# Where tasks stand in a hand-written order: weight fetches, word sums and splits between three fused stages

## The chip, the cores and the metric

One Trainium2 chip, one of its cores. The metric is the device time of one execution in microseconds (us); the kernel before was run three times, and its median is what the changed kernel is compared with.

## The reference, cut to what matters

Decayed linear attention over 12 blocks (written as chunks of 128 tokens in the kernel), then two MLPs on its 1536 x 512 output:

```
x   = attention(q, k, v, lam)                    # 2 batches x 768 tokens, 8 heads of 64
h   = x @ w_in                                    # 512 -> 2048
x   = (s * relu(h)**2 + b) @ w_out                # 2048 -> 512           (MLP1)
xn  = x / sqrt(mean(x*x) + 1e-6) * rms_g
x   = (silu(xn @ w_gate) * (xn @ w_val)) @ w_out  # 512 -> 1536 -> 512    (MLP2)
```

The weights come as 64-bit numbers.

## The kernel before, in words

**Words.** A weight piece is fetched as raw 64-bit words into one of two rooms (`stage[0]`, `stage[1]`, by SP's queue, line 116). ScalarE makes a float from the upper word (`scale_word`, L123) and reads the low word (`low_word`, L129); VectorE shifts (L135) and adds the two (`sum_words`, L140). Then a matrix is split into a high part (`split_hi`, ScalarE, L143) and a low part (`split_lo`, VectorE, L146), and each product is three matmul passes (`PASSES`), hi x hi, hi x lo, lo x hi.

**Seven products.** The first matmul of each MLP is done in quads: a weight pair `j` and a half of the tokens (batch) `s`, as Strassen-Winograd 2 x 2 blocks with seven products instead of eight. Sums of weight blocks (S1 to S4) are made on GpSimd (L218 to L221), sums of x blocks (T1 to T4) on VectorE (L267); all are split. A quad is five parts with a `yield` after each; the additions between products are VectorE's (L306, `add`). A product that goes on top of a bank can start only after the addition that reads the bank. The weights 0 and 1 of MLP1 use eight plain products (`hplain`).

**Tasks.** `w_tasks(j, after)` gives the tasks of one weight pair in order: `first` (scale and low word of the first half, then `after(0)`, which issues the fetch of the next pair's first half), `second`, `third` (then `after(1)`), `sums_hi` (GpSimd's four sums, then the split of blocks that need no sum), `first_lo` (their low part, then ScalarE's split of S1 to S4) and `second_lo` (two low parts). Weights 0 and 1 of MLP1 have five tasks (`plain_hi`, `plain_lo` at the end); weights 2 to 7 seven (`fourth` and `first_hi` apart). `x_tasks` gives t1 to t4 and the high and low part of each x block (hB11, lB11, ...).

All engines work through their instructions in the order in which the program issues them; that order is written by hand. Three mechanisms set it:

- In the attention, `plan[g]` says which tasks are issued after chunk `g`'s outputs, then `load_chunk(g + 4)` issues that chunk's q, k, v. All loads and fetches are issued on SP's queue, in this order; a fetch waits there until its room has been read.
- In MLP1's first matmul, `plan[(i, part)]` says which tasks follow part `part` of quad `i`; MLP2's first matmul has another such plan.
- Between them, MLP1's second matmul runs over 16 f tiles for each of two token halves (`blk`): step `it` makes the `y_product` and `z_product` of f tile m for four columns d. The operand of tile m is split three steps ahead (`r_hi(m + 3)`, `r_lo(m + 3)`) into one of four rooms. In the second half, the list `todo` holds the tasks for MLP2: weights 8 and 9, 18 x tasks, weights 10 and 11; `work(n)` issues the next n of them. Only the first 12 f tiles run in this loop; the last four run column by column (`for d in range(NK)`), so that each column's `square` (ScalarE) and `take1` (VectorE) follow while the next column is computed.

In MLP2's loop over quads, `work()` is called after the parts 1, 3 and 4 and issues one task of `todo` each.

Of the kernel before, what the change touches and what calls it, by code (L numbers as in the profile page):

```python
# [22 lines left out]
def attention_moe_moe2_kernel(  # L23
# [83 lines left out]
    def work(n=1):  # L107
        for _ in range(min(n, len(todo))):
            todo.pop(0)()
# [327 lines left out]
    with tc.tile_pool(name="att", bufs=1) as att:  # L437
# [20 lines left out]
        NPRE = 4  # L458
        nc.vector.memset(ones, 1.0)
        row = att.tile([1, H + 2], F32, name="row")  # L460
        nc.scalar.dma_start(row[:, 0:H], lam.rearrange("(o h) -> o h", o=1))
        load_qk(0)
        load_qk(1)
        load_v(0)
# [137 lines left out]
        prepare(0)  # L602
        def after_w(j):
            def load(part):
                if j + 1 < 2:
                    load_w(j + 1, part)

            return load

# [3 lines left out]
        def spread_s():  # L613
# [3 lines left out]
            nc.vector.tensor_copy(params[:, H : H + 2], pps[:, 0:2])  # L617

        plan = {
            3: w0[0:1], 4: w0[1:2], 5: w0[2:4] + [xt["hB11"]],  # L620
            6: [xt["lB11"]], 7: [xt["hB21"]] + w0[4:5], 8: [xt["lB21"], xt["hB12"]],
            9: [xt["lB12"], xt["hB22"]], 10: [xt["lB22"]] + w1[0:1], 11: w1[1:2] + [spread_s],
        }
        for g in range(NG):
            if (g + 1) % NCH == 0 and g + 1 < NG:
                prepare_state(g + 1)
            if g + 1 < NG:
                prepare(g + 1)
            if g % NCH:
                prepare_state(g)  # L630
            if g == NG - 1:

                quad0 = hquad(0)
                next(quad0)
                next(quad0)
            st = outputs(g)
            add_state(g, st)
            scores(g + 2)
            for t in plan.get(g, ()):
                t()  # L640
            load_chunk(g + NPRE)
            if g == 1:
                load_w(0, 0)
                load_w(0, 1)
            if g == 8:
                nc.sync.dma_start(g_col, rms_g.rearrange("(k p) -> p k", p=P))
                nc.sync.dma_start(row[:, H : H + 1], s.rearrange("(o h) -> o h", o=1))
                nc.sync.dma_start(row[:, H + 1 : H + 2], b.rearrange("(o h) -> o h", o=1))
# [19 lines left out]

        return load

    load_w(2, 0)
    load_w(2, 1)
    wt = {j: w_tasks(j, next_w(j)) for j in range(2, NPR)}
    wo = {f: out1_tasks(f) for f in range(NF1)}

# [10 lines left out]
    def r_lo(m):  # L686
# [14 lines left out]
        (3, 0): [ut["lT3"], wt[2][4]],  # L701
        (3, 1): [wt[2][5]],
        (3, 2): [wt[2][6]],
        (3, 3): [wt[3][0]],
        (4, 0): [ut["hT4"]],
        (4, 1): [ut["lT4"]],
    }
    for ts, slots in (
        (wt[3][1:], ((4, 1), (4, 2), (4, 3), (5, 1), (5, 2), (5, 3))),
        (wt[4], ((5, 4), (6, 1), (6, 2), (6, 3), (7, 1), (7, 2), (7, 3))),  # L710
        (wt[5], ((7, 4), (8, 1), (8, 2), (8, 3), (9, 1), (9, 2), (9, 3))),
        (wt[6], ((9, 4), (10, 1), (10, 1), (10, 2), (10, 3), (10, 4), (11, 1))),
# [75 lines left out]
    for blk in range(B):  # L788
# [42 lines left out]
            take(d, xq[blk][:, d, BT:BW], acc2[d // 2][:, d % 2 * BX : (d % 2 + 1) * BX])  # L831


        by_f = NF1 if blk == 0 else NF1 - 4
        for it in range(by_f):
            m = NF1 * blk + it
            if m == 0:
# [24 lines left out]
            if it == 0:  # L862
                norm_total(0)
                m_u0[0] = piece(early, "u0a", 12)
                ops2.append([x_place(m_u0[1], i) for i in range(5)] + [x_place(m_u0[0], i) for i in range(2)])

                def next_w2(j):
                    def load(part):
                        if j + 1 < NPR + NF2:
                            load_w(j + 1, part)  # L870

                    return load

                w2 = [w_tasks(NPR + f, next_w2(NPR + f)) for f in range(NF2)]
                xt = x_tasks(xq[0], ops2[0], xq[1])
                todo += w2[0] + w2[1] + [xt[k] for k in X_ORDER] + w2[2] + w2[3]
            if it == 1:
                norm_rstd(0, bank(0, "nps0"))
            if it in (3, 4):
# [1 line left out]
                norm_apply(0, slice(h * HB, (h + 1) * HB), bank(1 - h, f"rb0_{h}")[:, 0:HB])()  # L881
            work(1)
            r_lo(m + 3)
            work((0, 0, 1, 1, 2, 2, 4, 4, 4, 4, 3, 1)[it])
        if blk == 0:
            for d in (0, 2):
                take1(d)
# [4 lines left out]
                square(NK + d)  # L892
            for d in range(NK):
                take2(d)
    r_hi(2 * NF1 - 1)
    r_lo(2 * NF1 - 1)
    for d in range(NK):
        for m in range(2 * NF1 - 4, 2 * NF1):
            y_product(m, d)
        for m in range(2 * NF1 - 4, 2 * NF1):  # L900
            z_product(m, d)
        square(d)
        if d == 0:
            work(2)
        take1(d)
        if d == 1:
            square(NK)
            square(NK + 1)
            take2(0)
            take2(1)  # L910
            work(1)
        if d == 2:
            work(len(todo))
            norm_pair(1, 0)


# [116 lines left out]
    def spread():  # L1033
# [5 lines left out]
        (0, 0): [lambda: square(NK + 2), lambda: square(NK + 3), lambda: take2(2), lambda: take2(3)],  # L1039
        (0, 1): [lambda: norm_pair(1, 2)],  # L1040
        (0, 2): [lambda: norm_pairs(1)],
        (0, 4): [lambda: norm_rstd(1, bank(1, "nps1"))],
        (1, 3): [spread],
        (1, 4): [lambda: scale[1]()],
        (2, 0): [xt["t1"], xt["hB11"]],
        (2, 1): [xt["t2"], xt["lB11"]],
        (2, 2): [xt["hT2"], xt["t3"]],
        (2, 3): [xt["lT2"], xt["hT3"]],
        (2, 4): [xt["hT1"]],
        (3, 0): [xt["lT3"]],  # L1050
        (3, 1): [xt["lT1"], xt["hB21"]],
        (3, 2): [xt["t4"]],
        (3, 3): [xt["hT4"], xt["lB21"]],
        (3, 4): [xt["hB22"]],
        (4, 0): [xt["lT4"]],
        (4, 1): [xt["lB22"]],
        (23, 1): [lambda: split_first(0)],
    }
    work(len(todo))
    for i in range(len(order)):  # L1060
        for part, _ in enumerate(quad(i)):
            for t in plan.get((i, part), ()):
# [123 lines left out]
```

## Time and profile before

| | |
|---|---|
| median of 3 runs | 614.34 us (614.27 to 614.41) |
| the profiled execution | 614.62 us; its span, first to last instruction, 612.7 us |
| TensorE busy | 592.5 us, 97% of the span |
| VectorE, ScalarE, GpSimd busy | 67%, 53%, 18% |
| mean granted clock of TensorE | 0.988 |

Times in the rows below are microseconds from the span's start. A row of the timeline can hold several like instructions (xN); in brackets stands how long the engine was idle before it and who ended that. PE is TensorE, DVE VectorE, ACT ScalarE, POOL GpSimd, SPq SP's queue. PEclk is the granted clock of TensorE, 1.00 for 2.4 GHz and 0.50 for 1.2 GHz. Durations on PE overlap their neighbours; the distance of two starts is the time that the work takes.

### The profile page before, as it was taken

Reading aid. Unit: us, or ns where it says so; the run is one execution under the profiler, and the core shown is the slowest. Engines: PE = TensorE matmul, PEld = TensorE weight load, DVE = VectorE, ACT = ScalarE, POOL = GpSimd, SP = SyncE. Lnnn points to the kernel's source line nnn. Section 1 sums busy time; section 2 is a strip of 40 time slices with the busy share of each in tenths; the row PEclk is TensorE's granted clock in tenths of the full one; section 3 lists DMA queues with packets and bytes.
Section 4 is the critical chain, followed back from the end, with each engine's and each line's share of the span. In section 5 each row is a group of like instructions: output and inputs, shape, how many; then the busy total and the mean of one; then the engine's idle time right before and its main releaser. Section 6 shows DMA issues by size and latency. Waiting matters only on the chain.

```text
span 612.7 us, 9214 instructions
## 1 busy us (share of the span) xinstructions
PE 592.5 (97%) x3590; PEld 546.0 (89%) x3590; DVE 408.9 (67%) x654; ACT 322.7 (53%) x572; POOL 111.8 (18%) x118
## 2 busy tenths in 40 slices
PE   8999799999999999999979989999999999999997
PEld 7888699999998888888858989999999998888886
DVE  5684785777777776668856696777777777875200
ACT  5674686678776664534643243444444445764200
POOL 3551021121122332032130100222222200000000
PEclk9999799999999999999979999999999999999999
DMA  8982102222232332112220001222222221330300
GB/s 324 339 301 70 35 34 70 70 70 74 92 110 74 135 138 68 35 35 68 69 69 1 2 1 35 76 80 85 70 68 70 70 68 58 115 103 1 137 35 35
DMA packets 17282, 51.98 MB, mean 85 GB/s; under 512 B 2390, under 2 KB 2390, under 8 KB 17238
## 3 DMA queue, kind: packets, MB, share of 16 engines
q1 hardware_dynamic: 17236, 51.39, 24.5%
q8 instruction: 28, 0.46, 0.3%
q14 instruction: 16, 0.13, 0.1%
q10 hardware_dynamic: 2, 0.00, 0.0%
HBM read 48.24 MB, written 3.15 MB: 84 GB/s over the span
## 4 chain that ended last, share of the span: by engine, by line
PE 81%; DVE 8%; ACT 4%; issue 2%; DMA 2%; POOL 1%; SPq 0%; DVEq 0%; ACTq 0%; POOLq 0%
PE q L295 26%; PE out L1078 16%; PE h L295 15%; PE y L794 11%; PE z L806 6%; PE o L557 1%; PE sc L515 1%; PE o L566 1%; DVE u_None L140 1%; DMA st_None<-in_w_dram 1%; ACT u_None L143 1%; DMA k<-in_kT_dram 1%; PE st L583 1%; DVE u_None L146 1%; DVE st_None L146 1%
## 5 line engine op out<-in xcount | busy, mean ns | idle before, releaser
L143 ACT ACTIVATE u_None<-u_None 128x768 fp32r<-128x768 f32 (+2 forms) x50 | 43.1, 870 | 52.8 <-DVE u_None L140 44.3
L295 PE MATMUL q<-u0b_None,u_None 128*128 128x384 f32 x360 | 68.6, 336 | 0.0
L295 PEld LDWEIGHTS q<-u0b_None,u_None 128*128 128x128 f32 x360 | 62.7, 188 | 0.9 <-DVE st_None L306 0.7
L146 DVE TENSOR_TENSOR u_None<-u_None,u_None 128x512 fp32r<-128x512 f32 (+1 forms) x66 | 53.7, 837 | 11.4 <-ACT u_None L143 11.4
L218 POOL TENSOR_TENSOR u_None<-u_None 128x256 f32<-128x256 f32 x18 | 19.7, 1094 | 208.8 <-DVE u_None L140 184.0
L123 ACT ACTIVATE u_None<-st_None 128x512 f32<-128x512 f32 x68 | 45.2, 665 | 19.7 <-issue 12.9
L295 PE MATMUL q<-xs_None,u_None 128*128 128x384 f32 x288 | 55.2, 334 | 0.0
L140 DVE CUSTOM_DVE_ANT_0 u_None<-u_None 128x1024 uint16<-128x1024 uint16 x68 | 47.3, 696 | 10.3 <-ACT u_None L129 5.3
L295 PEld LDWEIGHTS q<-xs_None,u_None 128*128 128x128 f32 x288 | 50.4, 188 | 0.0
L129 ACT ACTIVATE u_None<-st_None 128x512 uint32<-128x512 uint16 x68 | 45.2, 665 | 6.9 <-DVE u_None L146 5.9
L306 DVE TENSOR_TENSOR st_None<-q,r_None 128x384 f32<-128x384 f32 x48 | 26.6, 554 | 20.8 <-PE q L295 20.7
L972 ACT ACTIVATE st_None<-r_None 128x384 f32<-128x384 f32 x24 | 12.6, 526 | 45.8 <-DVE r_None L306 45.8
L135 DVE TENSOR_SCALAR u_None<-u_None 128x512 uint32<-128x512 uint32 x68 | 32.9, 484 | 1.1 <-ACT u_None L123 0.7
L1078 PE MATMUL out<-u_None,xs_None 128*128 128x512 f32 x144 | 32.8, 389 | 0.0
L1078 PEld LDWEIGHTS out<-u_None,xs_None 128*128 128x128 f32 x144 | 27.0, 188 | 5.6
L295 PE MATMUL q<-u0a_None,u_None 128*128 128x384 f32 x144 | 29.0, 336 | 1.7 <-DVE st_None L306 1.7
L295 PE MATMUL h<-u0b_None,st_None 128*128 128x384 f32 x126 | 26.2, 355 | 4.2 <-DVE st_None L146 2.3
L1085 DVE COPY st_None<-out 128x512 f32<-128x512 f32 x4 | 2.8, 692 | 40.9 <-PE out L1078 40.9
L424 POOL TENSOR_TENSOR wsum_None<-wsum_None,u_None 128x512 f32<-128x512 f32 x15 | 20.6, 1372 | 49.1 <-DVE u_None L140 49.1
L295 PEld LDWEIGHTS h<-u0b_None,st_None 128*128 128x128 f32 x126 | 23.5, 202 | 5.2 <-DVE st_None L146 2.6
L295 PEld LDWEIGHTS q<-u0a_None,u_None 128*128 128x128 f32 x144 | 25.2, 188 | 2.4 <-DVE st_None L306 2.4
L295 PE MATMUL q<-g_None,u_None 128*128 128x384 f32 x144 | 26.9, 334 | 0.0
(202 smaller groups left out, 1317.3 us busy)
## 6 DMA issues: line engine op xcount, KB each, us to landing
st_None<-in_w_dram SPq DMA_DIRECT2D x68, 512.0 KB, 3.3
kv<-in_kv_dram SPq DMA_DIRECT2D x12, 512.0 KB, 7.4
q<-in_qT_dram SPq DMA_DIRECT2D x12, 256.0 KB, 6.5
k<-in_kT_dram SPq DMA_DIRECT2D x12, 256.0 KB, 7.0
out_dram<-st_None SPq DMA_DIRECT2D x8, 256.0 KB, 2.2
out_dram<-u_None SPq DMA_DIRECT2D x4, 256.0 KB, 2.6
row<-in_lam_dram ACTq DMA_DIRECT2D x1, 0.0 KB
g_col<-in_rms_g_dram SPq DMA_DIRECT2D x1, 2.0 KB, 6.5
```

Source lines behind the costliest of these rows:

```text
L123: nc.scalar.activation(m, t[:, :, 1].bitcast(F32), AF.Prelu, scale=2.0**-112, alpha=-(2.0**32))
L129: nc.scalar.activation(to.bitcast(U32), low, AF.Copy, scale=2.0**-13)
L135: nc.vector.tensor_scalar(m, m, 3, None, op0=ALU.logical_shift_left)
L140: nc.vector.tensor_tensor(m, m, t.bitcast(U32), op=ALU.add)
L143: nc.scalar.activation(to, src, AF.Copy)
L146: nc.vector.tensor_tensor(to, src, hi.bitcast(F32), op=ALU.subtract)
L295: nc.tensor.matmul(ps, ws[:, wi, wop * KC + kt * P : wop * KC + (kt + 1) * P], xs[xop][:, xi, kt, :], start=n == 0 and not more, stop=n == ...
L306: nc.vector.tensor_tensor(to, ps, more, op=ALU.add)
L424: nc.gpsimd.tensor_tensor(wsum, wsum, m, op=ALU.add)
L794: nc.tensor.matmul(acc[d], wt[:, wi, d * P : (d + 1) * P], gt[:, gi, 0:BT], start=it == 0 and pi == 0, stop=it == NF1 - 1 and pi == 2,)
L806: nc.tensor.matmul(acc2[d // 2][:, d % 2 * BX : (d % 2 + 1) * BX], wt[:, wi, d * P : (d + 1) * P], gt[:, gi, BT:BW], start=it == 0 and pi ...
L1078: nc.tensor.matmul(ps, rows_[:, ai], w_out[f][:, wi, :], start=first and pi == 0, stop=last and pi == 2)
```

## The change

- lam is loaded on SP's queue instead of ScalarE's, ahead of all other loads.
- In the attention, the fetch of weight 0 moves from after chunk 1 to after chunk 4, and its tasks to chunks 6 to 9; the splits of x blocks move to chunks 4 to 10.
- The fetch of weight 2 was issued behind the attention, ahead of the third task of weight 1 (`w1[2]`) which reads the same room; now the tasks of weight 1 issue it themselves, each half after its room has been read.
- In MLP1's first matmul, T4's split and the tasks of weight 3 move one or more parts later.
- In MLP1's second matmul, the loop takes 13 f tiles and the rows by column three. The x tasks alternate with the tasks of weight 10, three x tasks and one weight task at a time; the number of tasks for each step becomes 2 (steps 0 to 5 and 12) or 4 (steps 6 to 11), one for each of the columns 0, 1 and 2, and one task of 42 is left for MLP2's loop.
- In MLP2's first matmul, the x tasks of the second token half move one part later each.

```diff
-        nc.scalar.dma_start(row[:, 0:H], lam.rearrange("(o h) -> o h", o=1))
+        nc.sync.dma_start(row[:, 0:H], lam.rearrange("(o h) -> o h", o=1))
...
-                if j + 1 < 2:
-                    load_w(j + 1, part)
+                load_w(j + 1, part)
...
         plan = {
-            3: w0[0:1], 4: w0[1:2], 5: w0[2:4] + [xt["hB11"]],
-            6: [xt["lB11"]], 7: [xt["hB21"]] + w0[4:5], 8: [xt["lB21"], xt["hB12"]],
-            9: [xt["lB12"], xt["hB22"]], 10: [xt["lB22"]] + w1[0:1], 11: w1[1:2] + [spread_s],
+            4: [xt["hB11"]], 5: [xt["lB11"], xt["hB21"]], 6: [xt["lB21"]] + w0[0:1], 7: [xt["hB12"]] + w0[1:2],
+            8: [xt["lB12"]] + w0[2:4], 9: [xt["hB22"]] + w0[4:5], 10: [xt["lB22"]] + w1[0:1], 11: w1[1:2] + [spread_s],
         }
...
-            if g == 1:
+            if g == 4:
                 load_w(0, 0)
                 load_w(0, 1)
...
-    load_w(2, 0)
-    load_w(2, 1)
...
-        (3, 3): [wt[3][0]],
-        (4, 0): [ut["hT4"]],
-        (4, 1): [ut["lT4"]],
+        (4, 1): [ut["hT4"]],
+        (4, 2): [ut["lT4"]],
     }
     for ts, slots in (
-        (wt[3][1:], ((4, 1), (4, 2), (4, 3), (5, 1), (5, 2), (5, 3))),
+        (wt[3], ((4, 2), (4, 3), (4, 3), (4, 4), (5, 1), (5, 2), (5, 3))),
...
-        by_f = NF1 if blk == 0 else NF1 - 4
+        by_f = NF1 if blk == 0 else NF1 - 3
...
-                todo += w2[0] + w2[1] + [xt[k] for k in X_ORDER] + w2[2] + w2[3]
+                todo += w2[0] + w2[1]
+                for i, t in enumerate(w2[2]):
+                    todo += [xt[k] for k in X_ORDER[3 * i : 3 * i + 3]] + [t]
+                todo += w2[3]
...
             work(1)
             r_lo(m + 3)
-            work((0, 0, 1, 1, 2, 2, 4, 4, 4, 4, 3, 1)[it])
+            work(1 if it < 6 or it > 11 else 3)
...
-    r_hi(2 * NF1 - 1)
-    r_lo(2 * NF1 - 1)
     for d in range(NK):
-        for m in range(2 * NF1 - 4, 2 * NF1):
+        for m in range(2 * NF1 - 3, 2 * NF1):
             y_product(m, d)
-        for m in range(2 * NF1 - 4, 2 * NF1):
+        for m in range(2 * NF1 - 3, 2 * NF1):
             z_product(m, d)
         square(d)
-        if d == 0:
-            work(2)
         take1(d)
+        if d < 3:
+            work()
         if d == 1:
             square(NK)
             square(NK + 1)
             take2(0)
             take2(1)
-            work(1)
         if d == 2:
-            work(len(todo))
             norm_pair(1, 0)
...
         (0, 2): [lambda: norm_pairs(1)],
+        (0, 3): [work],
...
-        (2, 0): [xt["t1"], xt["hB11"]],
-        (2, 1): [xt["t2"], xt["lB11"]],
-        (2, 2): [xt["hT2"], xt["t3"]],
-        (2, 3): [xt["lT2"], xt["hT3"]],
-        (2, 4): [xt["hT1"]],
-        (3, 0): [xt["lT3"]],
-        (3, 1): [xt["lT1"], xt["hB21"]],
...
+        (2, 0): [xt["hB11"]],
+        (2, 1): [xt["t1"]],
+        (2, 2): [xt["lB11"], xt["t2"]],
+        (2, 3): [xt["hT2"], xt["t3"]],
+        (2, 4): [xt["lT2"], xt["hT3"]],
+        (3, 0): [xt["hT1"]],
+        (3, 1): [xt["lT3"]],
+        (3, 2): [xt["lT1"], xt["hB21"]],
...
-    work(len(todo))
     for i in range(len(order)):
```

## Rows read from the trace of the kernel before

**Rows 1.** The page: busy time, share and instructions of each engine.
```profile
PE 592.5 (97%) x3590; PEld 546.0 (89%) x3590; DVE 408.9 (67%) x654; ACT 322.7 (53%) x572; POOL 111.8 (18%) x118
```

**Rows 2.** Stretches: length, busy us (x instructions) per engine, PEclk, DMA share, GB/s.
```profile
57.50:75.46 17.96, 13.72 (x60) 13.08 (x61) 11.26 (x15) 12.32 (x20) 0.74 (x1) 0.81 0.19 59
...
305.41:330.23 24.82, 20.54 (x99) 16.77 (x98) 13.80 (x19) 11.30 (x16) 6.20 (x7) 0.86 0.14 44
```

**Rows 3.** Timeline, MLP1's last f tiles: start, length, engine, line, operation [idle before].
```profile
301.23 2.91 PE L794 MATMUL y<-st_None,xs_None 128*128 128x512 f32 x12
...
308.14 1.06 ACT L143 ACTIVATE u_None<-u_None 128x1024 fp32r<-128x1024 f32 x1 [2.13 <-POOL u_None L221]
309.11 0.83 ACT L143 ACTIVATE st_None<-u_None 128x768 fp32r<-128x768 f32 x1
...
309.98 0.51 PE L794 MATMUL y<-st_None,g_None 128*128 128x512 f32 x1 [3.03 <-ACT st_None L143]
...
330.23 2.25 PE L295 MATMUL q<-u0b_None,u_None 128*128 128x384 f32 x12
```

**Rows 4.** Timeline, VectorE and TensorE before and in MLP2's first quads.
```profile
326.36 1.28 DVE L146 TENSOR_TENSOR u_None<-u_None,u_None 128x512 fp32r<-128x512 f32 x2
...
335.15 0.55 DVE L306 TENSOR_TENSOR st_None<-q,r_None 128x384 f32<-128x384 f32 x1
...
338.24 1.39 PE L757 MATMUL nps<-ones,xq_None 128*128 128x1 f32 x12
...
355.10 1.32 PE L295 MATMUL q<-u0a_None,u_None 128*128 128x384 f32 x6 [1.58 <-DVE st_None L306]
```

**Rows 5.** Timeline, MLP1's first quad of seven products and its next.
```profile
100.53 1.32 PE L295 MATMUL h<-u0a_None,u_None 128*128 128x384 f32 x6 [0.99 <-DVE u_None L306]
...
102.83 1.20 PE L295 MATMUL h<-xs_None,u_None 128*128 128x384 f32 x6
...
103.87 2.24 PE L295 MATMUL h<-g_None,u_None 128*128 128x384 f32 x12
```

**Rows 6.** Timeline, MLP1's first quads: the last pieces of weight 1.
```profile
61.35 0.66 ACT L129 ACTIVATE u_None<-st_None 128x512 uint32<-128x512 uint16 x1 [0.95 <-DMA st_None<-in_w_dram]
...
63.88 0.61 PE L295 MATMUL h<-u0b_None,st_None 128*128 128x384 f32 x2 [1.92 <-ACT st_None L143]
...
66.81 3.57 PE L295 MATMUL h<-u0b_None,st_None 128*128 128x384 f32 x10 [2.32 <-DVE st_None L146]
```

**Rows 7.** Timeline, attention.
```profile
19.98 1.09 PE L557 MATMUL o<-prob,kv 128*64 128x128 f32 x16
...
23.80 1.09 PE L557 MATMUL o<-prob,kv 128*64 128x128 f32 x16
...
24.82 0.42 SPq L445 DMA_DIRECT2D k<-in_kT_dram  x1
...
30.38 1.16 PE L515 MATMUL sc<-q,k 64*128 64x128 f32 x16 [0.58 <-DMA k<-in_kT_dram]
...
34.78 1.06 ACT L143 ACTIVATE u_None<-u_None 128x1024 fp32r<-128x1024 f32 x1 [3.76 <-DVE u_None L140]
...
50.39 2.35 PE L295 MATMUL h<-u0b_None,u_None 128*128 128x384 f32 x12
```

**Rows 8.** Groups by line, 8 to 50.4 us: xcount | busy us, mean ns | idle.
```profile
L534 ACT ACTIVATE kdec<-kv,dec 128x64 f32<-128x64 f32 x80 | 20.0, 336 | 5.5 <-DVE dec L487 5.4
L517 DVE TENSOR_TENSOR prob<-sc,dec 128x512 f32<-128x512 f32 x24 | 15.5, 686 | 1.5 <-PE sc L515 0.7
...
L577 ACT ACTIVATE xq_None<-o 128x512 f32<-128x512 f32 x11 | 6.5, 589 | 6.5 <-PE o L566 6.5
...
L140 DVE CUSTOM_DVE_ANT_0 u_None<-u_None 128x1024 uint16<-128x1024 uint16 x2 | 1.4, 692 | 0.3
```

**Rows 9.** Line 135 (VectorE's shift), durations of all: least/median/most in ns.
```profile
L135 DVE TENSOR_SCALAR u_None<-u_None x68: 414/421/1266, 28.9 to 555.5; 128x512 uint32<-128x512 uint32 x68
```

**Rows 10.** Timeline, the first product with the values.
```profile
9.18 0.43 PE L557 MATMUL o<-prob,kv 128*64 128x128 f32 x2 [1.18 <-DVE prob L517]
```

More of the change, by code (lines that the diff above doesn't have):

```diff
@@ L1044, in attention_moe_moe2_kernel @@
         (1, 4): [lambda: scale[1]()],
-        (2, 0): [xt["t1"], xt["hB11"]],
-        (2, 1): [xt["t2"], xt["lB11"]],
-        (2, 2): [xt["hT2"], xt["t3"]],
-        (2, 3): [xt["lT2"], xt["hT3"]],
-        (2, 4): [xt["hT1"]],
-        (3, 0): [xt["lT3"]],
-        (3, 1): [xt["lT1"], xt["hB21"]],
[L1052 to L1056, printed above, removed]
+        (2, 0): [xt["hB11"]],
[6 more added lines that the diff above has]
+        (3, 2): [xt["lT1"], xt["hB21"]],
+        (3, 3): [xt["t4"]],
+        (3, 4): [xt["hT4"], xt["lB21"]],
+        (4, 0): [xt["hB22"]],
+        (4, 1): [xt["lT4"]],
+        (4, 2): [xt["lB22"]],
         (23, 1): [lambda: split_first(0)],
     }
-    work(len(todo))
     for i in range(len(order)):
```

## The prediction

> **What bounds the kernel now.** I read the page first: TensorE is busy 97% of the span, VectorE 67% [rows 1]. So an edit pays only where TensorE stands still, or where its clock is down. The timeline of TensorE, filtered for lines with idle time ahead of them, gives four such places, and the view by stretches says what the clock did there. (a) The last four f tiles of the first MLP's second projection, 305.41 to 330.23: TensorE waits 3.03 us for ScalarE, and the granted clock is 0.86 on average [rows 2, 3]. (b) The start of MLP1, 57.50 to 75.46: waits of 1.92 and 2.32 us, clock 0.81 [rows 2, 6]. (c) The first quad of seven products, 0.99 us [rows 5], and a quad of MLP2, 1.58 us [rows 4]. (d) The attention, where chunks that should follow each other at 3.82 us stretch after 30 us [rows 7]. Everywhere else TensorE is the bound, and its work is not changed.
>
> **The last f tiles.** One f tile takes 4.18 us when nothing waits (301.23 to 305.41), four take 16.72; the stage takes 24.82 [rows 2, 3]. So 8.10 us are lost: 3.03 are the one long wait, the rest shorter waits for VectorE and the matmuls at 1.2 instead of 2.4 GHz (a mean of 0.86 over 24.82 us is 6.9 us at the lower level). The cause is in ScalarE's order. The wait for `r_hi(30)` (309.11) is not a wait for its data: ahead of it stands the split of weight 10's sums, which sat 2.13 us until GpSimd's last sum was there [rows 3]. `r_hi(31)` is issued later still, only behind the loop.
> After the change the loop runs 13 f tiles, so `r_hi(31)` is issued at 305.4 and wanted at 311 or later (305.41 + 4.18, and two f tiles of one of the four columns, 0.73 each by the 2.91). The sums of weight 10 are issued at the end of step 9 and their split at the end of step 10, one step of 4.18 us between them, where now one follows the other. In step 11 ScalarE holds only `r_hi(30)` and one split, 1.7 us; VectorE holds three subtractions and `second_lo`, 0.96 x 3 + 1.28 = 4.2 us (1.28 is two of 512 columns, so 768 are 0.96 [rows 4]), as much as the step, but `r_lo(30)` is the first of them and has two steps of slack. Steps 0 to 5 take two tasks each; `first_hi` of weight 8 writes room that `r_lo(20)` reads, and `r_lo(20)` is issued before it. I take the whole 8.10 us: the row by columns then ends at 322.13.
>
> **What is late next.** The last task, `second_lo` of weight 11 (1.28 us on VectorE, [rows 4]), is now popped in MLP2's first quad, between `norm_pair` and the addition that frees bank 2. That addition starts 4.92 us after the quad's start now (335.15 less 330.23), and the quad takes 8.01 (to 338.24) [rows 3, 4]. With the task ahead of it TensorE waits up to 1.28 more; I take 1.2, since the takes before it come a little earlier.
> In the quad that waits 1.58, `t1` moves behind the addition to u2, `t2` and the low part of B11 move behind the addition that TensorE waited for. That wait goes; but the two (0.96 each) now stand ahead of the next addition, and by 4.92 + 1.9 + 0.6 for itself it ends 7.4 us into the quad instead of the 6.2 to 6.6 that TensorE needs, so some 0.8 of the 1.58 come back at the last product. Net 0.8.
> Sum for the tail and MLP2's start: 8.1 - 1.2 + 0.8 = 7.7 us.
>
> **The first quad of seven products.** There VectorE does T4's low part and the word sums of weight 3 before the addition that TensorE waits for. Both move behind it. The two products after the wait start 2.30 us before the next quad (100.53 to 102.83) where six matmuls take 1.04 (102.83 to 103.87), so 0.99 + 2.30 - 2.08 = 1.2 us are lost [rows 5]. Weight 3 is needed two quads later; its sums end some 1 us later in a quad of 7.3. Gain 1.2 us.
>
> **The fetch of weight 2.** `w1[2]` reads its low word at 61.35 after 0.95 us of waiting for a fetch of weight 2 that was issued ahead of it into the same room [rows 6]. After the change the fetch comes behind the read. The chain behind it (sum, split, first matmuls at 63.88, low parts, 66.81) moves by 0.95. The two waits stay otherwise. Weight 2's second half is read only in the next quad, so its later fetch stays hidden; uncovered it would cost a landing, 5.6 at most by the k tile of [rows 7].
> The clock: 19% of 17.96 us at the lower level means 6.8 us at 1.2 GHz, about 5.8 of them behind 66.81 [rows 2, 6]. These cost 2.9 us. With 0.95 less of waiting the clock may stay up. I assume that it falls as before, so nothing for it.
>
> **The attention.** Now SP holds chunk 7's loads until ScalarE has read weight 0's low word; the k tile issued at 24.82 lands at 30.38, 5.6 us later, with TensorE waiting [rows 7]. ScalarE then waits 3.76 us in the order for VectorE's word sum [rows 7]. From 23.80, seven chunks of 3.82 would end at 50.54; chunks 5, 6 and 10 lack parts, some 2.8 us by the matmul rows of 1.1, so 47.8 would be the floor against 50.39 [rows 7]. At most 2.6 us can be had.
> After the change the same hold sits two chunks later. By these chunk lengths chunk 5 starts at 27.6, chunk 8 at 37.3. ScalarE does copy 5, B21, kdec 7, copy 6 and two words from 29.8 on: 0.59 + 0.83 + 2.0 + 0.59 + 1.32, the word is read at about 35 [rows 3, 6, 8]. Chunk 10's k goes out 0.9 later and lands, by the 5.6, at 41.3; it is wanted 2.7 into chunk 8, at 40.0. Scores, their product (1.37), B12's low part (0.96), shift (0.42) and sum (0.69) then end near 45.8; ScalarE splits (1.06), makes kdec 10 (2.0), and copies 9, B22 and 10 (2.0), and that last copy frees the bank of MLP1's first product: 50.4, taking 0.1 off each for the overlap of neighbours [rows 3, 7, 8, 9]. So I take no change: 0. With chunk 10 in time it is 49.2 (1.2 won). With the shift at its longest, 1.27 [rows 9], 51.2 (0.8 lost).
> The first of the 68 shifts lies in the attention, and the longest takes three times the median [rows 9]. By the Trainium skill (SBUF — State Buffer, section "SBUF: two separate sides") VectorE and GpSimd share one port pair as an exclusive lock, so such a shift is blocked for GpSimd's whole instruction. By that rule it would be the 51.2; by the median of the row, 0.421, the 50.4 above. The trace agrees as far as this one long row goes.
>
> **lam on SP's queue.** One more issue ahead of all loads, 0.4 us by SP's rows [rows 7]. The first product with the values waits 1.18 us for VectorE's decayed scores [rows 10], and these wait for scans of lam, not for q and k. Hidden: 0; uncovered it would cost 0.4.
> The Trainium skill (Trainium Kernel Development and Optimization, "Key Constraints") says that DMAs of all queues run on the same engines and that several issuers only save issue time; by that the move costs 0.4 at SP and wins nothing. No row here shows lam landing.
>
> **The sum.** 7.7 + 1.2 + 0.95 + 0 = 9.9 us off 614.62, the profiled execution (span 612.7 and 1.9 around it): 604.7. The median of the runs shown is 0.28 lower: 604.4.
>
> **The rivals.** 1. MLP1's clock stays up: for it, the waits shrink from 4.24 to 3.3 us; against it, the two are only 0.6 us of matmul apart [rows 6]. 604.4 - 2.9 = 601.5. 2. VectorE's backlog is larger: the sums of weight 11 on GpSimd end later than I think, `second_lo` waits for the split, and quads 0 to 2 lose another 1.3 us or two, with the attention's 0.8: 606.5 to 607. For it, VectorE was the one late in both waits of MLP2. 3. The change doesn't do what it says at the f tiles: the split of weight 10 still blocks ScalarE past 309.6. Issued near 297, the four sums would have to end past 309, while now ScalarE waits 2.13 for them [rows 3]. Then only the small gains stay: 612.5. 4. The other side: weight 0's fetch, issued at about 27 behind chunk 8's loads, holds ScalarE and, behind it, chunk 10. The end of the attention follows the low word by some 15.5 us. From a word read at 45 on the loss eats all gains; landed at 47, the time is 616. It would take a landing of 18 us or more, against 5.6 in that stretch [rows 7].
>
> **How the numbers follow.** Forecast 0.59 (602.9 to 606), rival 1 0.18, rival 2 0.14, rival 3 0.06, rival 4 0.03. The range 601.0 to 607.5 takes in the first three with the attention's bounds. Within 0.2% (1.2 us, about what a measurement here can tell from none) needs rival 3 at its worst: 0.03; slower 0.03; faster 0.94.
>
> **What would show it.** TensorE without idle time from 301 to 322, clock 1.00 there; no wait for DMA ahead of L129 in MLP1's first quads; no wait in the first quad of seven products; in MLP2's first quad a wait near 1.3 us longer; chunk 10's scores waiting for k. The prediction is wrong if the f tiles still wait, or if quads 0 to 3 lose more than 3 us.

## The result and the profile after

The changed kernel takes 605.73 us (median of 4 runs, 603.99 to 606.62); the kernel before, run beside it on the same chip, 614.38 (614.27 to 614.62). The ratio is 0.9855, with a 95% interval from 0.9831 to 0.9879. The profiled execution of the changed kernel took 606.62 us with a span of 604.7.

The page's busy row says little again, as a row of averages will: TensorE lost 4.3 us of busy time against [rows 1], which is mostly clock and not work, since the instructions are the same 3590 and the mean granted clock rose from 0.988 to 0.994.

```profile
PE 588.2 (97%) x3590; PEld 544.0 (90%) x3590; DVE 407.9 (67%) x654; ACT 321.9 (53%) x572; POOL 112.1 (19%) x118
```

**The last f tiles.** The view by stretches of the changed kernel, with the columns of [rows 2]: MLP1's first quad, its two next, the last four f tiles, MLP2's quad 0.

```profile
51.72:60.40 8.68, 8.43 (x50) 7.80 (x50) 1.83 (x4) 1.61 (x4) 0.00 (x0) 0.80 0.17 60
60.40:76.60 16.20, 13.02 (x63) 12.38 (x64) 11.27 (x15) 12.42 (x21) 0.69 (x1) 0.89 0.20 66
304.90:321.64 16.74, 16.74 (x98) 14.76 (x97) 8.91 (x15) 8.81 (x13) 2.86 (x4) 1.00 0.19 64
321.64:330.86 9.22, 7.84 (x44) 7.20 (x43) 7.02 (x12) 1.90 (x4) 0.00 (x0) 1.00 0.00 0
```

The third row answers [rows 2]: the stage fell from 24.82 to 16.74 us, TensorE is busy for all of it, and the clock is 1.00 instead of 0.86. The timeline shows why, against [rows 3]:

```profile
299.10 1.45 POOL L221 TENSOR_TENSOR u_None<-u_None 128x256 f32<-128x256 f32 x1
...
300.58 1.06 ACT L143 ACTIVATE u_None<-u_None 128x1024 fp32r<-128x1024 f32 x1 [1.20 <-POOL u_None L221]
301.55 0.83 ACT L143 ACTIVATE st_None<-u_None 128x768 fp32r<-128x768 f32 x1
...
305.10 0.85 ACT L143 ACTIVATE st_None<-u_None 128x768 fp32r<-128x768 f32 x1 [1.99 <-PE z L801]
...
309.78 1.53 PE L789 MATMUL y<-st_None,g_None 128*128 128x512 f32 x6
...
321.64 2.25 PE L295 MATMUL q<-u0b_None,u_None 128*128 128x384 f32 x12
```

ScalarE still waits 1.20 us for GpSimd's last sum, but now at 299.4, with `r_hi(30)` behind it done at 302.38 and `r_hi(31)` at 305.95. TensorE takes the first of them at 309.78 and waits for neither.

**MLP2's first quads**, the timeline against [rows 4]:

```profile
325.70 0.95 DVE L738 TENSOR_TENSOR xq_None<-xq_None 128x768 f32<-128x768 f32 x1
326.57 1.29 DVE L146 TENSOR_TENSOR u_None<-u_None,u_None 128x512 fp32r<-128x512 f32 x2
327.77 0.55 DVE L306 TENSOR_TENSOR st_None<-q,r_None 128x384 f32<-128x384 f32 x1
...
328.38 1.32 PE L295 MATMUL q<-u0a_None,u_None 128*128 128x384 f32 x6 [1.36 <-DVE st_None L306]
...
330.86 1.39 PE L752 MATMUL nps<-ones,xq_None 128*128 128x1 f32 x12
...
348.19 2.01 PE L295 MATMUL q<-u0b_None,u_None 128*128 128x384 f32 x10 [0.88 <-DVE st_None L306]
```

The last task of weight 11 (326.57) stands between `norm_pair` and the addition that TensorE needs, so quad 0 takes 9.22 us where it took 8.01. Two quads on, the wait of 1.58 is 0.88, one product later.

**MLP1's first quad of seven products**, against [rows 5]: 7.28 us from its start to the next quad's, with no wait inside.

```profile
94.92 2.24 PE L295 MATMUL h<-u0b_None,u_None 128*128 128x384 f32 x12
...
102.20 1.20 PE L295 MATMUL h<-xs_None,u_None 128*128 128x384 f32 x6
```

**MLP1's start**, against [rows 6]:

```profile
63.17 0.66 ACT L129 ACTIVATE u_None<-st_None 128x512 uint32<-128x512 uint16 x1
...
65.70 0.62 PE L295 MATMUL h<-u0b_None,st_None 128*128 128x384 f32 x2 [0.87 <-ACT st_None L143]
...
68.64 3.25 PE L295 MATMUL h<-u0b_None,st_None 128*128 128x384 f32 x10 [2.31 <-DVE st_None L146]
```

ScalarE reads the low word without waiting for a DMA, and TensorE's first wait shrinks by 1.05; the second is what it was.

**The attention**, against [rows 7, 9, 10]:

```profile
9.10 0.43 PE L557 MATMUL o<-prob,kv 128*64 128x128 f32 x2 [1.73 <-DVE prob L517]
...
35.80 0.42 SPq L445 DMA_DIRECT2D k<-in_kT_dram  x1
...
41.64 1.16 PE L515 MATMUL sc<-q,k 64*128 64x128 f32 x16 [1.69 <-DMA k<-in_kT_dram]
...
44.87 0.42 DVE L135 TENSOR_SCALAR u_None<-u_None 128x512 uint32<-128x512 uint32 x1
...
44.99 1.43 POOL L529 TENSOR_TENSOR qs<-q,lpow 128x512 f32<-128x512 f32 x1 [2.86 <-PE o L566]
...
45.43 1.54 DVE L140 CUSTOM_DVE_ANT_0 u_None<-u_None 128x1024 uint16<-128x1024 uint16 x1
...
47.01 1.06 ACT L143 ACTIVATE u_None<-u_None 128x1024 fp32r<-128x1024 f32 x1 [5.75 <-DVE u_None L140]
...
51.72 3.91 PE L295 MATMUL h<-u0b_None,u_None 128*128 128x384 f32 x12 [1.36 <-ACT xq_None L577]
```

Read it upwards: MLP1's first product waits for ScalarE's copy of chunk 10, ScalarE stood 5.75 us in front of a split whose word sum VectorE ends at 46.97, and VectorE came to that sum late because chunk 10's scores had waited 1.69 us for a k tile issued at 35.80. The first product follows the first product with the values by 42.62 us, where it was 50.39 less 9.18 = 41.21 [rows 7, 10]. The twelve matmuls at 51.72 take 3.91 us instead of 2.35: the clock was at the lower level here, from 51.9 to 55.4.

**Where the time went, by stages.** In the table, the distances between five starts of TensorE in each profile: A is the first product with the values, B from there to MLP1's first product, C from there to the third quad of MLP1, D from there to MLP2's first product, E its quad 0 (to `nps`), F the rest of the span.

| | A | B | C | D | E | F | span |
|---|---|---|---|---|---|---|---|
| before | 9.18 | 41.21 | 27.15 | 252.69 | 8.01 | 274.46 | 612.7 |
| after | 9.10 | 42.62 | 26.56 | 243.36 | 9.22 | 273.84 | 604.7 |
| again | 9.79 | 42.51 | 25.00 | 243.33 | 9.23 | 273.84 | 603.7 |

`again` is a second profile of the changed kernel (below). D, E and F agree between the two within 0.03 us; A and C do not. So the tail's gain is firm, and what varies from one execution to the next lies before 80 us.

### The profile page after: what moved, and what is told of

Read it like the earlier page. It is cut to its first block, busy times and chain, and to the rows that moved or that the text cites. A ratio compares the mean times of both kernels' runs of the same rounds, so it can differ in the third digit from the quotient of the medians.

```text
span 604.7 us, 9212 instructions
## 1 busy us (share of the span) xinstructions
PE 588.2 (97%) x3590; PEld 544.0 (90%) x3590; DVE 407.9 (67%) x654; ACT 321.9 (53%) x572; POOL 112.1 (19%) x118
## 4 chain that ended last, share of the span: by engine, by line
PE 87%; DVE 5%; ACT 4%; issue 2%; DMA 1%; SPq 0%; DVEq 0%
PE q L295 27%; PE h L295 17%; PE out L1073 16%; PE y L789 15%; PE z L801 8%; PE o L557 1%; PE sc L515 1%; PE o L566 1%; DMA k<-in_kT_dram 1%; DVE u_None L140 1%; ACT kdec L534 1%; PE warm L479 1%; DVE r_None L306 1%; PE st L583 0%; DVE u_None L146 0%
## 5 line engine op out<-in xcount | busy, mean ns | idle before, releaser
L295 PEld LDWEIGHTS q<-xs_None,u_None 128*128 128x128 f32 x288 | 50.4, 188 | 0.0
L135 DVE TENSOR_SCALAR u_None<-u_None 128x512 uint32<-128x512 uint32 x68 | 30.2, 444 | 1.1 <-ACT u_None L123 0.7
L295 PE MATMUL h<-u0b_None,u_None 128*128 128x384 f32 x126 | 25.8, 353 | 1.6 <-ACT xq_None L577 1.4
```

The costliest lines, as they stand in the source:

```text
L135: nc.vector.tensor_scalar(m, m, 3, None, op0=ALU.logical_shift_left)
L295: nc.tensor.matmul(ps, ws[:, wi, wop * KC + kt * P : wop * KC + (kt + 1) * P], xs[xop][:, xi, kt, :], start=n == 0 and not more, stop=n == ...
```

## The experiments

Each experiment changes the changed kernel and nothing else, unless its diff says so. The first four ran beside one another on one chip (the kernel before took 614.15 there, 612.71 to 615.06), the next four on one (614.38, 613.57 to 615.68), the last three on one (614.08, 612.26 to 614.39). Ratios are to these.

| run | us, median (range) | ratio [95%] | B | C | D | E |
|---|---|---|---|---|---|---|
| again | 605.60 (604.10 to 606.63) | 0.9862 [0.9840, 0.9883] | 42.51 | 25.00 | 243.33 | 9.23 |
| attn_back | 604.55 (604.08 to 605.00) | 0.9847 [0.9830, 0.9864] | 41.22 | 25.02 | 243.33 | 9.24 |
| loads_first | 603.83 (603.65 to 604.20) | 0.9836 [0.9820, 0.9853] | 41.02 | 25.01 | 243.34 | 9.23 |
| last_task | 603.97 (603.58 to 604.38) | 0.9838 [0.9821, 0.9854] | 42.47 | 24.99 | 243.32 | 8.03 |
| tail_back | 612.44 (611.49 to 613.47) | 0.9966 [0.9953, 0.9980] | 43.14 | 24.88 | 251.32 | 8.01 |
| x_first | 606.77 (605.41 to 607.15) | 0.9870 [0.9854, 0.9885] | 42.94 | 26.20 | 243.33 | 9.22 |
| four_rows | 605.07 (602.30 to 606.29) | 0.9843 [0.9823, 0.9864] | 41.88 | 25.00 | 243.40 | 9.48 |
| lo_first | 603.07 (602.09 to 603.72) | 0.9814 [0.9799, 0.9830] | 42.30 | 21.82 | 243.30 | 9.22 |
| early_words | 602.97 (602.40 to 603.50) | 0.9823 [0.9806, 0.9840] | 39.75 | 25.89 | 243.30 | 9.24 |
| best3 | 598.25 (598.10 to 598.31) | 0.9746 [0.9731, 0.9761] | 39.84 | 21.83 | 243.35 | 8.01 |
| lam_act | 604.79 (604.13 to 606.09) | 0.9856 [0.9833, 0.9879] | 41.97 | 25.02 | 243.33 | 9.24 |

**again: the changed kernel, once more.** No edit.

> The changed kernel once more, for a second trace and more times. Its four times so far lie 603.99 to 606.62, those of before within 0.35 us. If the landing of chunk 10's k tile varies, this trace shows another wait ahead of its scores than 1.69 us; if it is the clock alone, the same wait and another place or length of the lower clock between 50 and 74 us. The median should be 605.0 to 606.5 either way.

605.60 us, as at first. The timeline of TensorE shows the same two waits at the attention's end as the first profile of this kernel:

```profile
42.23 1.16 PE L515 MATMUL sc<-q,k 64*128 64x128 f32 x16 [1.58 <-DMA k<-in_kT_dram]
...
52.30 2.35 PE L295 MATMUL h<-u0b_None,u_None 128*128 128x384 f32 x12 [1.36 <-ACT xq_None L577]
```

But the twelve matmuls behind them take 2.35 us here, not 3.91: the lower clock of the first profile in MLP1's first quad comes and goes (no other profile below has it there). It cost 1.56 us (C: 26.56 less 25.00).

**attn_back: the attention's task order as before.**

```diff
-            4: [xt["hB11"]], 5: [xt["lB11"], xt["hB21"]], 6: [xt["lB21"]] + w0[0:1], 7: [xt["hB12"]] + w0[1:2],
-            8: [xt["lB12"]] + w0[2:4], 9: [xt["hB22"]] + w0[4:5], 10: [xt["lB22"]] + w1[0:1], 11: w1[1:2] + [spread_s],
+            3: w0[0:1], 4: w0[1:2], 5: w0[2:4] + [xt["hB11"]],
+            6: [xt["lB11"]], 7: [xt["hB21"]] + w0[4:5], 8: [xt["lB21"], xt["hB12"]],
+            9: [xt["lB12"], xt["hB22"]], 10: [xt["lB22"]] + w1[0:1], 11: w1[1:2] + [spread_s],
...
-            if g == 4:
+            if g == 1:
```

> The attention's plan and the fetch of weight 0 as before; all else as changed. Theory (the later fetch costs time, 1.3 us at the attention's end, and lets the clock fall ahead of MLP1): MLP1's first product at 50.4 again, no lower clock before 62 us, time 602.5 to 604.0. Rival (what the attention loses is regained, because the lower stretch of the clock only moves): MLP1's third quad starts within 0.5 us of the changed kernel's 78.3, time 605 to 606.5.

B is 41.22, that of the kernel before (41.21) to 0.01 us, and C stays at 25.02. So the attention's new order costs 1.3 us (42.51 less 41.22), and nothing of it is paid back in MLP1's first quads. The size is uncertain: in the eight profiles that have this order of the attention, B lies anywhere from 41.88 to 43.14. The median, 604.55, lies above the range expected, and the intervals of the two ratios overlap, so this price rests on B and not on the median.

**loads_first: each chunk's loads issued ahead of its tasks.**

```diff
+            load_chunk(g + NPRE)
             for t in plan.get(g, ()):
                 t()
-            load_chunk(g + NPRE)
```

> As changed, but each chunk's loads are issued ahead of the tasks of that chunk, so that SP no longer holds chunk 10's loads behind the fetch that waits for ScalarE. Theory (the hold is the cause): the wait of 1.69 us for chunk 10's k is gone, VectorE's word sum and the copies behind it come 1.7 us earlier or more, MLP1's first product at 49.3 to 50.1, time 601.5 to 604. Rival (the DMA engines are the bound, the same bytes in the same stretch): a wait of over 1 us stays at the scores of chunk 10 or 11, time 605 to 606.5.

No chunk waits for a k tile any more, and B falls by 1.49 to 41.02. The second wait stays:

```profile
45.79 1.06 ACT L143 ACTIVATE u_None<-u_None 128x1024 fp32r<-128x1024 f32 x1 [4.13 <-DVE u_None L140]
...
50.50 2.38 PE L295 MATMUL h<-u0b_None,u_None 128*128 128x384 f32 x12 [1.36 <-ACT xq_None L577]
```

So there are two stalls in the attention, one behind the other: SP's hold of chunk 10's loads, and ScalarE's split standing in its order ahead of kdec 10 and two copies. Taking the first away lets the second set the end, which is why the first product comes at 50.50, 0.4 later than expected.

**last_task: the last task of weight 11 behind column 3, not in MLP2's first quad.**

```diff
-        if d < 3:
-            work()
+        work()
```

> As changed, but the last task (second_lo of weight 11) is issued after the last column's take1 instead of in MLP2's first quad. Theory (VectorE's order: it stands ahead of the addition that frees bank 2): it fills VectorE's gap between take1(3) and take2(2), the wait of 1.36 us in MLP2's first quad falls to 0.2 or less, time 1.2 us below the changed kernel's. Rival (the takes of the last column, which wait for ScalarE's squares, set that addition): the wait stays over 1 us, time unchanged.

E falls from 9.23 to 8.03, TensorE's wait from 1.36 to 0.16:

```profile
326.09 1.33 PE L295 MATMUL q<-u0a_None,u_None 128*128 128x384 f32 x6 [0.16 <-DVE st_None L306]
```

So the 1.2 us that the prediction put on this task are all of the wait that it causes, and were not needed.

**tail_back: MLP1's last f tiles as before,** with the order of the tasks, twelve steps, the counts of each step and the row of four. The rest of the change stays.

```diff
-        by_f = NF1 if blk == 0 else NF1 - 3
+        by_f = NF1 if blk == 0 else NF1 - 4
...
-                todo += w2[0] + w2[1]
-                for i, t in enumerate(w2[2]):
-                    todo += [xt[k] for k in X_ORDER[3 * i : 3 * i + 3]] + [t]
-                todo += w2[3]
+                todo += w2[0] + w2[1] + [xt[k] for k in X_ORDER] + w2[2] + w2[3]
...
-            work(1 if it < 6 or it > 11 else 3)
+            work((0, 0, 1, 1, 2, 2, 4, 4, 4, 4, 3, 1)[it])
...
+    r_hi(2 * NF1 - 1)
+    r_lo(2 * NF1 - 1)
...
-        for m in range(2 * NF1 - 3, 2 * NF1):
+        for m in range(2 * NF1 - 4, 2 * NF1):
...
+        if d == 0:
+            work(2)
         take1(d)
-        if d < 3:
-            work()
...
+            work(1)
...
+            work(len(todo))
```

> As changed, but MLP1's second matmul as before: 12 f tiles in the loop, four by column, the x tasks ahead of weight 10's, the old number of tasks a step, all tasks issued ahead of MLP2. Theory (the f tiles carry nearly the whole gain: 8.1 us won there, 1.2 given back in MLP2's first quad): waits of 3 and 1 us at the f tiles again with the lower clock behind them, time 612 to 613. Rival (the gain comes from the whole order, the f tiles only a part of it): 608 to 610.

612.44 us. The chain of [rows 3] is back, 1.05 us earlier:

```profile
307.09 1.06 ACT L143 ACTIVATE u_None<-u_None 128x1024 fp32r<-128x1024 f32 x1 [2.13 <-POOL u_None L221]
...
308.94 0.50 PE L789 MATMUL y<-st_None,g_None 128*128 128x512 f32 x1 [3.02 <-ACT st_None L143]
```

D rises by 7.99 us and E falls by 1.22, together 6.77 of the 9.0 us by which the span of `again` is shorter than that of the kernel before. The ratios, 0.9966 against 0.9862, say the same: some three quarters of what the change brings come from this one stage.

**x_first and four_rows: which of the two edits at the f tiles does it?** `x_first` keeps the thirteenth step and the counts, and lets the x tasks stand ahead of weight 10's as before. `four_rows` keeps the alternation and the counts of the steps, and goes back to twelve steps and the row of four, with two, one and two tasks after its columns 0, 1 and 2.

```diff
# x_first
-                todo += w2[0] + w2[1]
-                for i, t in enumerate(w2[2]):
-                    todo += [xt[k] for k in X_ORDER[3 * i : 3 * i + 3]] + [t]
-                todo += w2[3]
+                todo += w2[0] + w2[1] + [xt[k] for k in X_ORDER] + w2[2] + w2[3]
# four_rows
-        by_f = NF1 if blk == 0 else NF1 - 3
+        by_f = NF1 if blk == 0 else NF1 - 4
...
+    r_hi(2 * NF1 - 1)
+    r_lo(2 * NF1 - 1)
     for d in range(NK):
-        for m in range(2 * NF1 - 3, 2 * NF1):
+        for m in range(2 * NF1 - 4, 2 * NF1):
...
+        if d == 0:
+            work(2)
         take1(d)
-        if d < 3:
-            work()
+        if 0 < d < 3:
+            work(d)
```

> As changed, with 13 f tiles in the loop, but the x tasks all ahead of the tasks of weight 10 as before. Theory A (the thirteenth step is what counts: r_hi(31) is issued in the loop, with time to spare): the split of weight 10's sums blocks ScalarE in step 11 behind r_hi(30), r_hi(31) ends near 310, TensorE waits 1 us or less, time 605.5 to 607. Theory B (the alternation is what counts, since the sums then have a step between issue and split): a wait of 3 us or more with the lower clock behind it, time 609 or more.

> As changed, with the alternating tasks, but 12 f tiles in the loop and four by column; r_hi(31) and r_lo(31) behind the loop, the same last task left for MLP2. Theory A (the thirteenth step counts): r_hi(31) comes too late by 2 us or more, the clock falls, time 608 or more. Theory B (the alternation counts): r_hi(30) no longer stands behind the split of the sums, r_lo(31) is there at 307.2 and wanted at 307.6, no wait over 0.5 us, time within 0.7 us of the changed kernel's 605.6.

D is 243.33 and 243.40, that of the changed kernel: either edit takes the whole stall away, with the new counts of tasks per step, which both runs keep. In `x_first` ScalarE waits for GpSimd as long as in [rows 3] (2.15 and 2.13 us), and it does no harm:

```profile
301.61 0.85 ACT L143 ACTIVATE st_None<-u_None 128x768 fp32r<-128x768 f32 x1 [0.71 <-PE z L801]
...
307.73 1.06 ACT L143 ACTIVATE u_None<-u_None 128x1024 fp32r<-128x1024 f32 x1 [2.15 <-POOL u_None L221]
308.69 0.83 ACT L143 ACTIVATE st_None<-u_None 128x768 fp32r<-128x768 f32 x1
...
310.40 1.53 PE L789 MATMUL y<-st_None,g_None 128*128 128x512 f32 x6
```

By the new counts the split of weight 10's sums is issued in step 11, behind `r_hi(30)` (301.61), where the kernel before issued it in step 10, ahead of it. So what it holds up is only `r_hi(31)` (308.69), and with a thirteenth step in the loop TensorE wants that later, behind tile 30. In `four_rows` the split of the sums is still ahead of `r_hi(30)`, and tile 31 is split behind the loop, but ScalarE's wait for GpSimd is 1.20 us and over at 298.89, so `r_hi(31)` starts at 303.42, in time too:

```profile
298.89 1.06 ACT L143 ACTIVATE u_None<-u_None 128x1024 fp32r<-128x1024 f32 x1 [1.20 <-POOL u_None L221]
...
303.42 0.85 ACT L143 ACTIVATE st_None<-u_None 128x768 fp32r<-128x768 f32 x1 [1.99 <-PE z L801]
```

No run has the new counts alone, or either edit with the old counts, so what the counts do by themselves is not shown. The medians differ from `again` by 1.2 and 0.5 us: `x_first` by C, where the clock was at the lower level from 67.2 to 74.1 us, `four_rows` by B (41.88; chunk 10 waited 0.47 us). No edit of either lies there.

**lo_first: weight 1's last low part ahead of three x tasks.** The wait of 2.3 us at MLP1's start is for `plain_lo` of weight 1, which stands behind x tasks on VectorE (in the first profile a sum from 64.48 and a low part from 66.42; it starts at 67.29).

```diff
-        (0, 2): [w1[2], w1[3], ut["hB11"], xt["t1"], ut["hB21"]],
-        (0, 3): [ut["lB11"], w1[4], ut["hB12"], ut["lB21"]],
+        (0, 2): [w1[2], w1[3], w1[4], ut["hB11"], xt["t1"], ut["hB21"]],
+        (0, 3): [ut["lB11"], ut["hB12"], ut["lB21"]],
```

> As changed, but in MLP1's first quad the last task of weight 1 (plain_lo) stands ahead of the x tasks t1, hB11 and lB11. Theory (TensorE's wait of 2.31 us there is VectorE's order, and the lower clock after it comes from the two waits): the wait falls to 1.0 or less, the clock between 66 and 73 us stays at 1.00, third quad 3 to 5 us earlier, time 601 to 603. Rival (the lower clock comes all the same, or the x operands are late in the third quad instead): under 2.0 us won, time 603.6 to 605.

```profile
65.83 2.00 PE L295 MATMUL h<-u0b_None,st_None 128*128 128x384 f32 x10 [0.71 <-DVE st_None L146]
...
60.00:78.00 18.00, 16.43 (x93) 15.78 (x93) 14.37 (x19) 16.36 (x27) 1.39 (x1) 1.00 0.18 59
```

The same stretch of `again`:

```profile
60.00:78.00 18.00, 14.82 (x76) 14.18 (x75) 12.58 (x17) 14.20 (x24) 0.74 (x1) 0.91 0.17 59
```

The wait falls by 1.60, and with it the lower clock goes: over 60 to 78 us it is 1.00, where `again` has 0.91. C falls by 3.18, twice the wait. The median falls by 2.5, as the clock stayed up in two of the five runs only (mean clock of the whole run 1.000; in the others 0.994 to 0.997).

**early_words: the loads first, weight 0 fetched after chunk 3, its first two words and its sum one chunk earlier, the split a chunk after the sum.**

```diff
-            4: [xt["hB11"]], 5: [xt["lB11"], xt["hB21"]], 6: [xt["lB21"]] + w0[0:1], 7: [xt["hB12"]] + w0[1:2],
-            8: [xt["lB12"]] + w0[2:4], 9: [xt["hB22"]] + w0[4:5], 10: [xt["lB22"]] + w1[0:1], 11: w1[1:2] + [spread_s],
+            4: [xt["hB11"]], 5: [xt["hB21"], xt["lB11"]] + w0[0:1], 6: [xt["lB21"]] + w0[1:2], 7: [xt["hB12"]] + w0[2:3],
+            8: w0[3:4] + [xt["lB12"]], 9: [xt["hB22"]] + w0[4:5], 10: [xt["lB22"]] + w1[0:1], 11: w1[1:2] + [spread_s],
...
+            load_chunk(g + NPRE)
             for t in plan.get(g, ()):
                 t()
-            load_chunk(g + NPRE)
-            if g == 4:
+            if g == 3:
```

> As changed, but each chunk's loads ahead of its tasks, weight 0 fetched after chunk 3, and its tasks spread over chunks 5 to 9 with the word sum of the second half a chunk behind its low word and ahead of B12's low part. Theory (two things delay the attention's end: SP's hold, and ScalarE waiting in order for VectorE's word sum): no wait for chunk 10's k, none for the copy ahead of MLP1's first product, that product 38.3 to 39.2 us after the first product with the values (42.5 as changed, 41.2 before), time 601.3 to 603. Rival (ScalarE has too much work in these chunks whatever the order): the wait for the copy stays over 1 us, time 603.5 or more.

```profile
39.82 1.13 PE L566 MATMUL o<-qs,state 128*128 128x128 f32 x8 [0.87 <-DVE state L596]
...
49.32 2.35 PE L295 MATMUL h<-u0b_None,u_None 128*128 128x384 f32 x12
```

Both stalls are gone. B is 39.75, 2.76 below `again` but above the 38.3 to 39.2 expected, with one new wait of 0.87 for a state sum.

**best3: early_words, last_task and lo_first together.**

> The three edits together: early_words, the last task after the last column, weight 1's plain_lo ahead of the x tasks. Theory (three separate waits, their prices add): 3 + 1.2 + 2.5 us below the changed kernel's 605.6, 598 to 600. Rival (they share one price, the lower clock at MLP1's start): 600.5 to 602.

```profile
63.13 2.01 PE L295 MATMUL h<-u0b_None,st_None 128*128 128x384 f32 x10 [0.71 <-DVE st_None L146]
...
320.08 1.32 PE L295 MATMUL q<-u0a_None,u_None 128*128 128x384 f32 x6 [0.15 <-DVE st_None L306]
```

598.25 us, 15.8 below the kernel before and 7.4 below the changed one. B, C and E are each what the single edits gave (39.84, 21.83, 8.01): the three prices add, since each lies on TensorE's own path. The clock stays at 1.00 or next to it in all runs (0.999 to 1.000), and the spread of four runs is 0.2 us.

**lam_act: lam on ScalarE's queue as before.**

```diff
-        nc.sync.dma_start(row[:, 0:H], lam.rearrange("(o h) -> o h", o=1))
+        nc.scalar.dma_start(row[:, 0:H], lam.rearrange("(o h) -> o h", o=1))
```

> As changed, but lam on ScalarE's queue again. Theory (hidden): the first product with the values starts as late as in the changed kernel's traces, 9.1 to 9.8 us, time 605 to 606.3. Rival (the issue ahead of all loads costs): 0.4 us earlier, time 604.5 to 605.3.

604.79, inside the spread of `again`. The median alone would fit the rival too, but A is 9.79 with either queue, so nothing moved that TensorE waits for; a price below what A itself varies (9.10 to 9.80 with lam on SP) can't be read from these runs.

## Why the prediction was right, and where its working failed

**The last f tiles: right in cause and size.** 8.10 us were predicted, 24.82 less 16.74 = 8.08 came. The cause given was ScalarE's order, a split that waits for GpSimd ahead of `r_hi(30)`, with `r_hi(31)` only behind the loop. `tail_back` shows the chain again with 3.02 us. What the prediction did not see is that, with the new counts, mending either half is enough: D is the same without the alternation (`x_first`) and without the thirteenth step (`four_rows`).

**What is late next: right.** 1.2 predicted and 1.21 measured for the last task in quad 0 (shown by `last_task`, which gives back 1.20); 0.8 predicted for the wait two quads on, 0.87 by the starts of the third quad (365.91 before, 357.66 after; 8.25 less the 7.38 at `nps`).

**The first quad of seven products: right,** 1.37 for 1.2. No run puts back this edit, the fetch of weight 2 or the x tasks of MLP2's quads alone; that they are the cause rests on the rows, where the wait named beforehand is gone or shorter. `tail_back`, which keeps the first, bears it out: there D is 1.37 below that of the kernel before (251.32 for 252.69).

**The fetch of weight 2: the wait right, its price too small.** The first wait fell by 1.05 where 0.95 was predicted. The step that failed is "I assume that it falls as before, so nothing for it". The clock did fall, but for half as long: 0.91 over 60 to 78 us in `again` is 3.2 us at the lower level, where 0.81 over 18 was 6.8. C fell by 2.15 (27.15 to 25.00), 1.1 more than the wait. That is the direction of rival 1, at some 40% of its 2.9. But the shorter stretch does not come every time: eight of the ten profiles with the new fetch and the old place of `plain_lo` have 3.4 us at the lower level there, `x_first` and `early_words` 6.9 as before, and in `x_first` C fell by 0.95 only, the bare wait. What decides it stays open. Over whole runs the clock rose too: the mean clock is 0.988 to 0.991 in all runs of the kernel before, 0.994 or 0.997 in all nine of the changed one, and of that the f tiles explain 6.9 us at the lower level out of 14.7 (1.2% of 612.7, twice).

**The attention: the mechanism right, the sum mis-sized, outside its own bounds.** Predicted was 0 with bounds from 1.2 won to 0.8 lost; 1.3 were lost (`attn_back`). The prediction foresaw the hold on SP's queue, chunk 10's k at 41.3 (it came at 41.64), and the copy that frees MLP1's bank. It ended VectorE's sum near 45.8; it ended at 46.97. Of the 1.2, 0.34 is the k tile, and 0.85 the sum itself: 1.54 us, priced at its mean of 0.69 [rows 8]. The upper bound stretched the shift by the longest of [rows 9], but kept the k tile at 41.3 and the sum at its mean. As it turned out the shift took 0.42, and it was the sum behind it that was stretched. A part of the k tile's 0.34 is a slip: the prediction's own terms, 35 and 0.9 and 5.6, add up to 41.5.

**lam: hidden,** as far as these runs can tell (`lam_act`).

**The sum.** Predicted 9.9, in the profiled execution 8.0. By stages, in us gained: f tiles and the quads of MLP2 7.7 as predicted (8.08 - 1.21 + 0.87), first quad of seven 1.37, weight 2's wait 1.05, the attention -1.41, the clock in MLP1's first quads -0.46 (1.10 won by the shorter stretch, 1.56 lost by the one at 51.9, which `again` hasn't), the start +0.08, small shifts of the rest -0.37. Without the stretch at 51.9, but with A 0.61 later, `again` gains 9.0. The point forecast is 1.3 below the median, about the attention's term; the shorter stretch of the lower clock, which the sum left out, and the 0.6 of the start make up for each other within a microsecond.

**The rivals.** Rival 2 (a larger backlog on VectorE) did not come: E and F are as the main case has them; only its attention part did. Rival 3 did not come; `tail_back` has its chain and nearly its time, 612.44 for 612.5, but by other terms (nothing lost in quad 0, more lost in the attention), so that agreement is chance. Rival 4 would have needed a landing of 18 us; weight 0's fetch was issued at 26.97, and ScalarE read its words from 33.38 on without a wait.

## What to carry to other kernels

When a task list is interleaved with a main loop, look for a task that waits for another engine and ask which of the main loop's own operands stands behind it on the same queue: here it was enough to have that task's producer done early (`four_rows`), or to put the task behind the operand that is wanted first and give the next one a step more (`x_first`). Price a task on VectorE by whether it falls beside an instruction of GpSimd, not by its mean. Its longest row is no safe bound either: the longest of the 68 word sums before took 1.01 us, and the one that counted here took 1.54, which was the rest of GpSimd's instruction (0.99) and 0.55 more. After the first large stall is gone, do the small waits of TensorE one by one, since in different stages their prices add (here 2.8, 3.2 and 1.2 us), and the one that brings the clock down can be worth twice its length (here 3.18 us for a wait shorter by 1.60).

## What the runs showed of the hardware

**VectorE beside GpSimd.** The word sum takes 0.69 us alone and 1.54 when GpSimd's product `qs` has started ahead of it: in the changed kernel `qs` runs from 44.99 to 46.42, and the sum, which starts at 45.43, ends at 46.97, 0.55 behind it. In the runs in which `qs` came later it is 0.69 in the same place, as in `last_task`:

```profile
46.73 0.69 DVE L140 CUSTOM_DVE_ANT_0 u_None<-u_None 128x1024 uint16<-128x1024 uint16 x1
...
47.67 1.28 POOL L529 TENSOR_TENSOR qs<-q,lpow 128x512 f32<-128x512 f32 x1 [4.83 <-PE o L566]
```

In the kernel before it was weight 0's two shifts that fell there: the first, from 28.93, is the longest of [rows 9], and the second, ahead of the sum that ScalarE waits for in [rows 7], ends 0.29 behind `qs`:

```profile
32.36 1.27 POOL L529 TENSOR_TENSOR qs<-q,lpow 128x512 f32<-128x512 f32 x1 [2.45 <-DMA q<-in_qT_dram]
...
32.76 1.16 DVE L135 TENSOR_SCALAR u_None<-u_None 128x512 uint32<-128x512 uint32 x1
```

So this chain had lost 0.74 us to GpSimd before the change and lost 0.85 after it, at another instruction. The Trainium skill (SBUF — State Buffer, section "SBUF: two separate sides") says that certain instructions of VectorE (in a mode that uses two ports, or with two inputs in SBUF against a GpSimd instruction that reads SBUF) and those of GpSimd hold the shared port pair in turn, each for its whole length, whichever starts first. The trace agrees, to the 0.14 between 0.55 and 0.69 for the sum, and to the 0.13 between 0.29 and 0.42 for the shift.

**The clock falls at different places from run to run.** The same kernel was at the lower level from 51.9 to 55.4 and from 69.0 to 72.4 us in one profile, and from 68.1 to 71.5 only in another. Four other profiles had a stretch at the lower level between 43 and 48 us; in these chunk 10's scores had waited 1.78, 2.29, 2.32 and 2.79 us for a DMA. `again`, with 1.58, had none there, nor had the first profile, with 1.69. Whether the wait is the cause was not tried by itself. A stretch inside the attention costs little by B, since `qs` then starts later, the sum takes 0.69 and the wait for the copy is nearly gone (`last_task`: B is 42.47 with a DMA wait of 2.29, `again` 42.51 with 1.58).

**The spread.** The kernel before spread over 612.3 to 615.7 us in these runs, the changed one over 604.0 to 606.6, `best3` over 0.2. Part of it is the clock (1.56 us for one stretch), part A, which was 9.10 in one profile of the changed kernel and 9.79 in the other; runs of it with the same mean clock of 0.997 still differ by 2.3 us (603.99 and 606.32), and what of it is the k tile's landing stays open.
